# A layer that opens in the place of another's weights, and a seventh product on a shared bank

## The chip, the cores and the metric

The kernel runs on 1 core of one Trainium2 chip. The metric is the device time of one execution in microseconds (us), smaller is better. The kernel before takes 1030.41 us, the median of three runs (1029.31 to 1032.5).

## The reference, cut to what matters

Three layers follow one another: windowed attention, a gated layer, and a two-matrix layer with the mish function. The first two stay as they are in this case; the third, and the passage into it, is what the change is about.

```python
def _moe_ref(x, w_gate, w_val, w_out):        # 2304 tokens, 512 -> 1536 -> 512
    g = x @ w_gate
    silu = g * (1.0 / (1.0 + np.exp(-g)))
    val = x @ w_val
    return (silu * val @ w_out).astype(np.float32)

def _moe2_ref(x, w_in, w_out):                # 2304 tokens, 512 -> 2048 -> 512
    h = x @ w_in
    sp = np.where(h > 20.0, h, np.log1p(np.exp(np.minimum(h, 20.0))))
    g = h * np.tanh(sp)
    return (g @ w_out).astype(np.float32)
```

## The kernel before

**Numbers.** Every matrix product is made of three TensorE matmuls of 128 rows: an operand is split into a high part (ScalarE copies it to the type fp32r, `hi_act`, L124) and a low part (VectorE subtracts the high part, `lo_dve`, L127), and high by high, high by low and low by high are summed in one PSUM bank (`mm`, L117).

**First layer.** It works through five token chunks. A chunk has groups of gate and value matmuls (24 of them, into `g_ps`) and projections of 12 matmuls that add to four accumulators `acc`. The weights that a projection needs pass through a ring of two tiles: SP loads `cw`, ScalarE and VectorE make the two parts `ring`. A projection runs some groups after its gate and value group; in the last chunk `CFG["lastlag"]` sets by how much, and four projections (48 matmuls) stand behind the last gate and value group. They are called `carry` in the code. Then `evacuate` (L580, L581) copies the accumulators out, and SP writes them to the DRAM tensor `x2d`. While the first layer runs, other code makes the seven combined weights of layer two's second matrix and SP writes them to DRAM (`w2o`, L556). Its twelve weight tiles `w` of 8 KB per partition, its activations and its ring lie in pools of one stack, `sa`, which is closed when the last projection has been issued. Only then does the pool `bp` of layer two open.

**Second layer.** `layer2` takes three blocks p of 768 tokens. Both matrix products are done with seven products of half-size blocks instead of eight (a scheme of Strassen's kind), numbered 1 to 7. `load_x` reads a block of tokens from `x2d` into `xr` (two loads, L682), `x_parts` makes seven operand pairs `xs1` to `xs7` with four VectorE sums (L666, in `sums4`) in between. In the hidden part, eight tiles j each do the seven products in `ORDER1`, 6 matmuls each, with weights `win` which `make_win` makes from a raw tile `w4` (L745): four subtractions on GpSimd (L752) into the only tile `t4`, then two ScalarE copies and two VectorE subtractions. `outputs` sums the banks into four quarters of `G` and `mish` is applied to each. In the output part each of the seven products in `ORDER2` has two banks (m = 0, 1) and four operands `op` (q = 0 to 3), each used by 6 matmuls on one bank and 6 on the other, 48 matmuls for a product. `operands` makes them from `G`, with four VectorE sums for each q, and five `op` buffers go round; `load_wout` brings the weights. `bank()` hands out alternately one of four rotating banks and one of the four accumulators in turn.

Product 2 is added onto product 1's bank, so that the sum of 1 and 2 needs no addition. The other sums are VectorE's. What `outputs` does with a product's bank is this:

```python
if i == 1:   u["a"] = new(); nc.scalar.activation(out=u["a"], in_=bk, func=AF.Copy)
elif i == 6: add(u["a"], u["a"], bk)
elif i == 7: u["b"] = new(); add(u["b"], u["a"], bk)
elif i == 2: done(0, bk, None)
elif i == 5: add(u["a"], u["a"], bk); done(3, u["b"], bk)
elif i == 3: done(1, u["a"], bk)
else:        done(2, u["b"], bk)
```

In the output part product 4 comes first; its two banks are kept until `b` is there, and `done(2, u["b"], p4)` is called after product 7 (tile `y`).

**What sets the order.** TensorE's instructions run in the order in which they are written. On the other engines and on the DMA queues a scheduler orders them when the program is built. All loads and stores spoken of here are on the queue of SP.

Of the kernel before, what the change touches and what calls it, by code (L numbers as in the profile page):

```python
# [9 lines left out]
F32 = mybir.dt.float32  # L10
F32R = mybir.dt.float32r
# [85 lines left out]
def body(ctx: ExitStack, tc: tile.TileContext, qT, kT, vP, w1, w1o, w2, cst, yT):  # L97
    nc = tc.nc
    const = ctx.enter_context(tc.tile_pool(name="const", bufs=1))
    sa = ExitStack()  # L100
    wp = sa.enter_context(tc.tile_pool(name="wp", bufs=12))
    xp = sa.enter_context(tc.tile_pool(name="xp", bufs=2))
    hp_ = sa.enter_context(tc.tile_pool(name="hp", bufs=2))
    dr = ctx.enter_context(tc.tile_pool(name="dr", bufs=1, space=bass.MemoryType.DRAM))
# [354 lines left out]
        return wp.tile([128, 2, 1024], F32R, tag="w", name="w")  # L459

    def ring_tile():
        return wp.tile([128, 2, 1024], F32R, tag="ring", name="ring", bufs=2)

    stage = {}

# [199 lines left out]
    def add(out, a, b, op=ALU.add):  # L665
        nc.vector.tensor_tensor(out=out, in0=a, in1=b, op=op)  # L666
# [68 lines left out]
    def layer2(bp, mish):  # L735
        G = {}
        win, wout = {}, {}
        ORDER1 = (1, 6, 7, 2, 5, 4, 3)
        ORDER2 = (4, 1, 6, 7, 2, 5, 3)

        raws = {}

        def load_raw(p, j):
            raws[p, j] = bp.tile([128, 4, 256], F32, tag="w4", name="w4", bufs=2)
            nc.sync.dma_start(out=raws[p, j], in_=w2d[j].rearrange("p (k n) -> p k n", k=4))  # L745

        def make_win(p, j):

            w = raws.pop((p, j))
            x = bp.tile([128, 4, 256], F32, tag="t4", name="t4", bufs=1)  # L750
            for o, a, b in ((0, w[:, 0], w[:, 1]), (1, w[:, 3], x[:, 0]), (2, w[:, 3], w[:, 0]), (3, x[:, 1], w[:, 2])):
                nc.gpsimd.tensor_tensor(out=x[:, o], in0=a, in1=b, op=ALU.subtract)  # L752
            t = win[p, j] = bp.tile([128, 2, 7, 256], F32R, tag="win", name="win")
# [9 lines left out]
        def hidden(p, j, xs):  # L763
            w = win.pop((p, j))
            q, jj = divmod(j, 2)
            if jj == 0:
                G[p, q] = bp.tile([128, 4, 2, TB], F32, tag=f"g{q}", name="G", bufs=1)
            g = G[p, q]
            u = {}

            def new():
                return bp.tile([128, TB], F32, tag="u", name="u", bufs=6)

            def done(k, a, b):
# [6 lines left out]
            bk1 = None  # L781
            for i in ORDER1:
                bk = bk1 if i == 2 else bank()
                if i == 1:
                    bk1 = bk
                s = SLOT[i]
                products(
                    bk, [(w[:, 0, s, c:c + 128], w[:, 1, s, c:c + 128]) for c in (0, 128)],
                    [(xs[i][:, 0, c], xs[i][:, 1, c]) for c in range(2)], i != 2, i != 1,
                )  # L790
                outputs(i, bk, u, new, done)

        def operands(p, i):

            ops = []
# [12 lines left out]

        xr = load_x(bp, 0)
        for j in range(2):  # L810
            load_raw(0, j)
        xs = x_parts(bp, xr)
        for j in range(2):
            make_win(0, j)
            load_raw(0, j + 2)
        yr = yT.rearrange("(c p) t -> p c t", p=128)
        for p in range(NPB):
            loads = [(i, k) for i in ORDER2 for k in range(2)]
# [6 lines left out]
                    load_wout(p, *loads.pop(0))  # L825
                hidden(p, j, xs)
            if p + 1 < NPB:
                xr = load_x(bp, p + 1)
# [4 lines left out]
            bk1 = [None, None]  # L833
            left = [[2, 2], [2, 2]]
            t0 = 2 * p * TB
            for i in ORDER2:
                bks = bk1 if i == 2 else [bank(), bank()]
                if i == 1:
                    bk1 = bks
                for q, o in enumerate(operands(p, i)):  # L840
                    k, jq = divmod(2 * q, NJ // 2)
                    if (p, i, k) not in wout:
# [5 lines left out]
                    for m in range(2):  # L848
                        products(
                            bks[m],  # L850
                            [(w[:, jq + e, 0, 128 * m:128 * m + 128], w[:, jq + e, 1, 128 * m:128 * m + 128]) for e in range(2)],
                            [(o[:, 0, e], o[:, 1, e]) for e in range(2)],
                            i != 2 and q == 0, i != 1 and q == NJ // 2 - 1,
                        )
                for m in range(2):

# [19 lines left out]
                        done(2, us[m]["b"], us[m]["p4"])  # L876
                if p + 1 < NPB:
                    if i == 7:
                        xs = x_parts(bp, xr)
                    if i in (2, 5):  # L880
                        j = (2, 5).index(i)
                        make_win(p + 1, j)
                        load_raw(p + 1, j + 2)

    with tc.manual_schedule(engines={mybir.EngineType.PE}):
# [42 lines left out]
        for ci, p in enumerate(plansA):  # L928
# [27 lines left out]
            for gi, (kind, i, f) in enumerate(groups):  # L956
# [12 lines left out]
                while win and (spent * ng < (gi + 1) * total or gi == len(groups) - 1):  # L969
# [23 lines left out]
        layer2(bp, mish)  # L993


def _layouts(np, q, k, v, moe_w_gate, moe_w_val, moe_w_out, moe2_w_in, moe2_w_out):
# [45 lines left out]
```

## Time and profile before

| what | value |
|---|---|
| runs | 1029.31, 1030.41, 1032.5 us (median 1030.41) |
| profiled execution, its own time | 1030.16 us |
| span of its profile | 1027.5 us |
| mean granted TensorE clock | 0.975 |
| TensorE busy with matmuls | 979.5 us, 5168 matmuls |
| attention and first layer, until the last projection ends | about 632.8 us |
| second layer | the rest |

The span runs from the first to the last recorded instruction; the execution's own time is 2.66 us longer. Engines are named PE (TensorE), DVE (VectorE), ACT (ScalarE), POOL (GpSimd) and SP (the queue that issues DMAs). A row of a timeline gives the start, the length, the engine, the line, the operation, what it writes and reads, how many instructions were put together, and in brackets how long the engine had been idle and which work released it.

### The profile page before, as it was taken

The numbers are of one execution on the slowest core, as the hardware profiler recorded it, in microseconds if no ns is written. First come the engines' busy times: TensorE is split into PE (matmuls) and PEld (weight loads), VectorE is DVE, ScalarE is ACT, GpSimd is POOL, SyncE is SP. The second block draws the span as 40 slices with busy tenths as digits, with TensorE's granted clock in tenths as the row PEclk, the third lists the DMA queues.
The fourth block names the chain that finished last, engine by engine and source line by source line (L and its number), as shares of the span: only waits on it lengthen the run. The fifth ranks groups of instructions, "written<-read, shape, count | busy, mean of one in ns | idle before, by whom it ended". The sixth has DMA issues, their size and how long they took to land.

```text
span 1027.5 us, 14547 instructions
## 1 busy us (share of the span) xinstructions
PE 979.5 (95%) x5168; PEld 860.0 (84%) x5168; DVE 722.6 (70%) x1271; ACT 551.4 (54%) x1121; POOL 151.6 (15%) x204
## 2 busy tenths in 40 slices
PE   7899999999999999999999996699899998999998
PEld 5567677898987777788888996599899998999998
DVE  5998887777667644468534573888984889758773
ACT  7867655757666754455443442455542565335442
POOL 3600000000000000000002440653221332113000
PEclk7899999999999999999999998699999999999999
DMA  8853424475345621247304995423586136850175
GB/s 317 278 206 128 154 85 129 147 238 184 121 145 172 217 91 60 78 155 246 123 1 147 355 326 179 191 83 103 189 290 218 62 126 226 285 171 32 55 256 202
DMA packets 74936, 173.90 MB, mean 169 GB/s; under 512 B 8432, under 2 KB 50032, under 8 KB 65136
## 3 DMA queue, kind: packets, MB, share of 16 engines
q1 hardware_dynamic: 74864, 172.98, 49.5%
q8 instruction: 40, 0.66, 0.2%
q14 instruction: 32, 0.26, 0.1%
HBM read 137.30 MB, written 35.65 MB: 168 GB/s over the span
## 4 chain that ended last, share of the span: by engine, by line
PE 76%; DVE 8%; DMA 6%; ACT 4%; issue 3%; POOL 2%; SPq 1%; DVEq 0%; ACTq 0%; POOLq 0%
PE g_ps L117 27%; PE bk L117 24%; PE acc L117 13%; PE o_ps L117 5%; PE s_ps L117 4%; PE t_ps L259 3%; DMA wraw<-w 2%; POOL t L752 2%; DVE G L666 2%; ACT win L124 1%; DVE win L127 1%; DVE op L127 1%; DMA wout<-w2o 1%; DVE xr L666 1%; DVE u L666 1%
## 5 line engine op out<-in xcount | busy, mean ns | idle before, releaser
L117 PE MATMUL g_ps<-xt,w 128*128 128x512 f32 (+1 forms) x1440 | 317.2, 371 | 0.3 <-ACT PT L271 0.3
L117 PEld LDWEIGHTS g_ps<-xt,w 128*128 128x128 f32 x1440 | 258.2, 188 | 37.6 <-issue 3.3
L117 PE MATMUL bk<-xs,win 128*128 128x384 f32 x1008 | 182.7, 340 | 22.0 <-ACT win L124 10.5
L117 PEld LDWEIGHTS bk<-xs,win 128*128 128x128 f32 x1008 | 177.0, 191 | 27.4 <-ACT win L124 10.8
L117 PE MATMUL bk<-op,wout 128*128 128x384 f32 x1008 | 179.7, 338 | 7.2 <-DVE op L127 6.4
L117 PEld LDWEIGHTS bk<-op,wout 128*128 128x128 f32 x1008 | 177.4, 191 | 9.1 <-DVE op L127 7.7
L117 PE MATMUL acc<-hh,ring 128*128 128x512 f32 (+1 forms) x480 | 149.5, 373 | 0.0
L124 ACT ACTIVATE op<-G 128x768 fp32r<-128x768 f32 x84 | 69.7, 842 | 64.9 <-PE bk L117 49.6
L127 DVE TENSOR_TENSOR op<-G,op 128x768 fp32r<-128x768 f32 x84 | 82.8, 999 | 26.0 <-ACT op L124 25.5
L117 PEld LDWEIGHTS acc<-hh,ring 128*128 128x128 f32 x480 | 89.1, 188 | 13.6 <-issue 1.9
L117 PE MATMUL acc<-hl,ring 128*128 128x512 f32 (+1 forms) x240 | 88.4, 368 | 0.0
L752 POOL TENSOR_TENSOR t<-w 128x256 f32<-128x256 f32 x48 | 48.6, 1034 | 236.7 <-DVE win L127 206.5
L230 ACT ACTIVATE Pt<-Pt,sm 128x256 f32<-128x256 f32 (+2 forms) x160 | 74.5, 467 | 16.9 <-DVE sm L226 16.6
L226 DVE CUSTOM_DVE_ANT_0 Pt<-s_ps,cst_sb 128x256 f32<-128x256 f32 (+2 forms) x160 | 54.5, 376 | 31.3 <-PE s_ps L117 31.0
L603 DVE SCALAR_TENSOR_TENSOR t<-t,g_ps 128x512 f32<-128x512 f32 (+1 forms) x60 | 37.7, 628 | 52.0 <-ACT t L602 51.9
L602 ACT ACTIVATE t<-g_ps 128x512 f32<-128x512 f32 (+1 forms) x60 | 33.0, 551 | 75.1 <-PE g_ps L117 74.9
L611 DVE SCALAR_TENSOR_TENSOR t<-t,g_ps 128x512 f32<-128x512 f32 (+1 forms) x60 | 37.9, 632 | 41.6 <-PE g_ps L117 40.9
L124 ACT ACTIVATE hh<-t 128x512 fp32r<-128x512 f32 (+1 forms) x60 | 34.9, 581 | 51.6 <-DVE t L611 51.6
L541 POOL TENSOR_TENSOR cw<-cw 128x256 f32<-128x256 f32 x32 | 30.0, 962 | 191.2 <-DMA cw<-w2d 163.8
L209 POOL MEMSET sm<- 128x8 f32 x40 | 4.9, 135 | 336.8 <-ACT Pt L247 308.7
L247 ACT ACTIVATE Pt<-Pt,sm 128x256 f32<-128x256 f32 (+2 forms) x128 | 50.2, 465 | 7.9 <-DVE sm L241 7.8
L666 DVE TENSOR_TENSOR u<-u,bk 128x384 f32<-128x384 f32 x72 | 39.6, 550 | 20.6 <-PE bk L117 18.8
(71 smaller groups left out, 1318.2 us busy)
## 6 DMA issues: line engine op xcount, KB each, us to landing
wout<-w2o SPq DMA_DIRECT2D x42, 1024.0 KB, 5.2
wraw<-w SPq DMA_DIRECT2D x16, 1024.0 KB, 5.6
w2o<-chl SPq DMA_DIRECT2D x16, 896.0 KB, 6.6
wst<-w SPq DMA_DIRECT2D x12, 1024.0 KB, 8.1
cw<-w1od SPq DMA_DIRECT2D x24, 512.0 KB, 3.9
w<-w2d SPq DMA_DIRECT2D x24, 512.0 KB, 3.2
w2d<-cw SPq DMA_DIRECT2D x16, 512.0 KB, 4.2
wraw<-w1o SPq DMA_DIRECT2D x6, 1024.0 KB, 6.4
```

The costliest lines, as they stand in the source:

```text
L117: nc.tensor.matmul(out=out, lhsT=lhsT, rhs=rhs, start=start, stop=stop, skip_group_check=True)
L124: nc.scalar.activation(out=out, in_=in_, func=AF.Copy)
L127: nc.vector.tensor_tensor(out=out, in0=in_, in1=hi.bitcast(F32), op=ALU.subtract)
L226: nc.vector.tensor_tensor_reduce(out=Pt[:q.qn, :w], in0=s_ps[:q.qn, q.so:q.so + w], in1=nb[:q.qn, 128 - q.kn:128 + q.qn], op0=ALU.add, op1 ...
L230: nc.scalar.activation(out=Pt[:q.qn, :w], in_=Pt[:q.qn, :w], func=AF.Exp, scale=-1.0, bias=sm[:q.qn, i:i + 1], accum_out=sm[:q.qn, 8 + i:9 ...
L247: nc.scalar.activation(out=pt, in_=pt, func=AF.Copy, scale=r)
L259: nc.tensor.transpose(t_ps[:x.n, o:o + q.qn], Pt[:q.qn, c0:c0 + x.n], ident[:q.qn, :q.qn])
L602: tanhs.append(nc.scalar.activation(out=t[:, :n], in_=st["g"][:, :n], func=AF.Tanh, scale=0.5))
L603: nc.vector.scalar_tensor_tensor(out=t[:, :n], in0=t[:, :n], scalar=1.0, in1=st["g"][:, :n], op0=ALU.add, op1=ALU.mult)
L611: nc.vector.scalar_tensor_tensor(out=t[:, :n], in0=t[:, :n], scalar=0.5, in1=vps[:, :n], op0=ALU.mult, op1=ALU.mult)
L666: nc.vector.tensor_tensor(out=out, in0=a, in1=b, op=op)
L752: nc.gpsimd.tensor_tensor(out=x[:, o], in0=a, in1=b, op=ALU.subtract)
```

## The change

1. `lastlag` goes from 3 to 4: five projections instead of four stand behind the last gate and value group.
2. The first layer's weight tiles get a stack of their own, `sw`, on the other side of the memory (`side="right"`); the ring moves to the pool of activations. As soon as the last gate and value group has been issued, `sw` is closed and in its place a pool `br` opens for layer two's `w4`, `t4`, `win`, `xr` and `xs`. `layer2` becomes a generator: its first part (the first loads, `x_parts`, `make_win` for two tiles) is issued before the `carry` projections, the rest after them, when `bp` has been opened.
3. Product 3 is added onto product 5's bank, as product 2 is onto product 1's (`onto`). The addition `add(u["a"], u["a"], bk)` after product 5 goes away: 24 times in the hidden part, 6 times in the output part. Product 5 comes before product 2 in both orders.
4. In `operands` the four sums for each q stand after product 4's, 1's and 7's operands and ahead of 6's, instead of three ahead of 6's and one ahead of 3's.

```diff
-    order="SSOTT", delay0=2, early=[4], pbufs=10, pump_g=2, pump_p=2, lag=4, lastlag=3, evprio=500,
+    order="SSOTT", delay0=2, early=[4], pbufs=10, pump_g=2, pump_p=2, lag=4, lastlag=4, evprio=500,
...
-    sa = ExitStack()
-    wp = sa.enter_context(tc.tile_pool(name="wp", bufs=12))
+    sa, sw = ExitStack(), ExitStack()
+    wp = sw.enter_context(tc.tile_pool(name="wp", bufs=12, side="right"))
...
         if i == 1:
-            u["a"] = new()
-            nc.scalar.activation(out=u["a"], in_=bk, func=AF.Copy)
+            u["c"] = new()
+            nc.scalar.activation(out=u["c"], in_=bk, func=AF.Copy)
         elif i == 6:
+            u["a"] = u.pop("c")
             add(u["a"], u["a"], bk)
...
+        elif i == 5:
+            done(3, u["b"], bk)
         elif i == 2:
             done(0, bk, None)
-        elif i == 5:
-            add(u["a"], u["a"], bk)
-            done(3, u["b"], bk)
...
-        ORDER1 = (1, 6, 7, 2, 5, 4, 3)
-        ORDER2 = (4, 1, 6, 7, 2, 5, 3)
+        ORDER1 = (1, 6, 7, 5, 2, 4, 3)
+        ORDER2 = (4, 1, 6, 7, 5, 2, 3)
+        onto = {2: 1, 3: 5}
...
                 if i == 6:
+                    add(g[:, 0], g[:, 3], g[:, 0], ALU.subtract)
+                part(o, g[:, {4: 3, 1: 0, 6: 0, 7: 2, 2: 1, 5: 3, 3: 2}[i]])
+                yield o
+                if i == 4:
                     add(g[:, 3], g[:, 2], g[:, 3])
+                if i == 1:
                     add(g[:, 2], g[:, 0], g[:, 2], ALU.subtract)
-                    add(g[:, 0], g[:, 3], g[:, 0], ALU.subtract)
-                if i == 3:
-                    add(g[:, 1], g[:, 1], g[:, 0], ALU.subtract)
-                part(o, g[:, {4: 3, 1: 0, 6: 0, 7: 2, 2: 1, 5: 3, 3: 1}[i]])
-                ops.append(o)
-                yield o
+                if i == 7:
+                    add(g[:, 2], g[:, 1], g[:, 0], ALU.subtract)
...
         pump(10000)
+        sw.close()
+        br = ctx.enter_context(tc.tile_pool(name="br", bufs=3, side="right", reuse_waits="tile"))
+        second = layer2(br)
+        next(second)
         for f in carry:
             f()
```

**SP's queue where the first layer ends.** `chl` holds combined output weights, `ev` the last evacuated sums. Before, the last `w2o` write is followed by the two writes to `x2d`, and only then by the loads for layer two:

```order
L556 DMA w2o_75<-chl_5913 128x7x256
L582 DMA x2d_72<-ev_6050 128x2x384
L582 DMA x2d_72<-ev_6054 128x2x384
L682 DMA xr_6066<-x2d_72 128x4x384 x2
L745 DMA w4_6069<-w2d_74 128x1024
L745 DMA w4_6071<-w2d_74 128x1024
L761 DMA wout_6498<-w2o_75 128x2048
```

Now:

```order
L556 DMA w2o_75<-chl_5884 128x7x256
L747 DMA w4_6006<-w2d_74 128x1024
L682 DMA xr_6008<-x2d_72 128x4x384 x2
L747 DMA w4_6011<-w2d_74 128x1024
L747 DMA w4_6048<-w2d_74 128x1024
L582 DMA x2d_72<-ev_6110 128x2x384
L747 DMA w4_6060<-w2d_74 128x1024
L582 DMA x2d_72<-ev_6114 128x2x384
```

The loads of `xr` and of the first raw weights have moved ahead of the last two writes to `x2d`.

**DVE at the same place.** `hl` is the low part of the last activation of layer one. Before:

```order
L127 TENSOR_TENSOR hl_5999<-t_5978,hh_5998 128x384
L581 COPY ev_6050<-acc1_5549 128x384
L581 COPY ev_6054<-acc3_5551 128x384
L127 TENSOR_TENSOR xs1_6073<-xr_6066,xs1_6073 128x768
L127 TENSOR_TENSOR xs2_6074<-xr_6066,xs2_6074 128x768
L127 TENSOR_TENSOR xs4_6076<-xr_6066,xs4_6076 128x768
L666 TENSOR_TENSOR xr_6066<-xr_6066 128x768
L127 TENSOR_TENSOR win_6103<-w4_6069,win_6103 128x768
```

Now:

```order
L127 TENSOR_TENSOR hl_5982<-t_5964,hh_5981 128x384
L127 TENSOR_TENSOR ring_5999<-cw_5997,ring_5999 128x1024
L127 TENSOR_TENSOR win_6043<-w4_6006,win_6043 128x768
L127 TENSOR_TENSOR xs1_6013<-xr_6008,xs1_6013 128x768
L127 TENSOR_TENSOR xs2_6014<-xr_6008,xs2_6014 128x768
L127 TENSOR_TENSOR win_6043<-t4_6038,win_6043 128x1024
L127 TENSOR_TENSOR xs4_6016<-xr_6008,xs4_6016 128x768
L581 COPY ev_6110<-acc1_5593 128x384
L666 TENSOR_TENSOR xr_6008<-xr_6008 128x768
L127 TENSOR_TENSOR win_6055<-w4_6011,win_6055 128x768
L581 COPY ev_6114<-acc3_5595 128x384
L666 TENSOR_TENSOR xr_6008<-xr_6008 128x768
```

Five operations for layer two and the last ring tile now stand ahead of the first evacuation. Behind these rows follow, in the kernel now, the low part of `xs5`, that of `win_6055` from `t4_6050`, a sum, that of `xs7`, a sum, and that of `xs6`.

**PE and DVE in the output part of block 0, from product 7 to the next.** Before, PE goes from product 7 (`bk_6915`, `bk_6916`) to product 2, on the banks of product 1:

```order
L117 MATMUL bk_6916<-op_6966,wout_6843 128x384 x6
L117 MATMUL bk_6765<-op_7012,wout_6881 128x384 [waits DMAHW4_49,Activation_49]
L117 MATMUL bk_6765<-op_7012,wout_6881 128x384 [waits DVE_49]
L117 MATMUL bk_6765<-op_7012,wout_6881 128x384 x4
L117 MATMUL bk_6766<-op_7012,wout_6881 128x384 x6
```

Now it goes to product 5, on two banks handed out anew (`bk_7004` is the accumulator that product 4 has held as `bk_6687`):

```order
L117 MATMUL bk_6903<-op_6956,wout_6836 128x384 x6
L117 MATMUL bk_7003<-op_7005,wout_6870 128x384 [waits DMAHW4_49,DVE_49,Activation_49]
L117 MATMUL bk_7003<-op_7005,wout_6870 128x384 [waits DVE_49]
L117 MATMUL bk_7003<-op_7005,wout_6870 128x384 x4
L117 MATMUL bk_7004<-op_7005,wout_6870 128x384 [waits DVE_49]
L117 MATMUL bk_7004<-op_7005,wout_6870 128x384 x5
```

The wait ahead of `bk_7004` is for the row that writes `y_6683` in DVE's order there:

```order
L127 TENSOR_TENSOR op_7054<-G_6554,op_7054 128x768
L666 TENSOR_TENSOR v_6972<-v_6826,bk_6902 128x384
L666 TENSOR_TENSOR v_6975<-v_6828,bk_6903 128x384
L127 TENSOR_TENSOR op_7083<-G_6137,op_7083 128x768
L666 TENSOR_TENSOR y_6682<-v_6972,bk_6686 128x384
L666 TENSOR_TENSOR y_6683<-v_6975,bk_6687 128x384
```

`op_7083` is the first operand of product 2, in the buffer that product 7's last operand `op_6956` leaves. Block 1 reads the same; in block 2 its row stands between the two `y`.

## Rows read from the trace of the kernel before

**Rows 1.** Page, part 1: busy time, share of the span, instructions.

```profile
PE 979.5 (95%) x5168; PEld 860.0 (84%) x5168; DVE 722.6 (70%) x1271; ACT 551.4 (54%) x1121; POOL 151.6 (15%) x204
```

**Rows 2.** Waits of PE from 650 us on: total us, times, longest us.

```profile
PE bk L117 <- DVE op L127: 6.4, 4, 2.5
PE bk L117 <- ACT u L719: 2.9, 7, 1.3
PE bk L117 <- DMA wout<-w2o: 0.8, 1, 0.8
```

**Rows 3.** PE's timeline at the passage between the layers.

```profile
632.45 0.34 PE L117 MATMUL acc<-hh,ring 128*128 128x384 f32 x1
643.32 1.01 PE L117 MATMUL bk<-xs,win 128*128 128x384 f32 x2 [10.53 <-ACT win L124]
...
655.17 11.51 PE L117 MATMUL bk<-xs,win 128*128 128x384 f32 x53 [3.24 <-DVE xs L127]
```

**Rows 4.** Windows: length, busy of PE, PEld, DVE, ACT, POOL, PEclk, DMA share, GB/s.

```profile
633.00:643.00 10.00, 0.00 (x0) 0.00 (x0) 3.17 (x4) 3.00 (x4) 0.47 (x1) 0.64 1.00 361
643.00:655.00 12.00, 3.34 (x7) 1.92 (x7) 11.99 (x10) 5.70 (x8) 8.15 (x7) 0.50 0.70 289
655.00:667.00 12.00, 11.51 (x53) 11.19 (x53) 8.53 (x12) 5.44 (x9) 6.98 (x8) 0.81 0.25 88
```

**Rows 5.** SP's timeline: the last w2o writes and the loads of xr.

```profile
605.87 10.69 SPq L556 DMA_DIRECT2D w2o<-chl  x4
...
633.90 1.29 SPq L682 DMA_DIRECT2D xr<-x2d  x2
```

**Rows 6.** ACT's timeline there.

```profile
638.98 1.58 ACT L124 ACTIVATE xs<-xr 128x768 fp32r<-128x768 f32 x2 [6.12 <-DMA xr<-x2d]
...
657.14 1.06 ACT L124 ACTIVATE win<-t 128x1024 fp32r<-128x1024 f32 x1 [2.55 <-POOL t L752]
```

**Rows 7.** The chain in order of time: start, us, what.

```profile
624.46 8.34 PE acc L117 x48
```

**Rows 8.** DVE's timeline at the passage.

```profile
631.78 0.56 DVE L581 COPY ev<-acc 128x384 f32<-128x384 f32 x1 [5.57 <-PE acc L117]
...
649.37 0.94 DVE L666 TENSOR_TENSOR xr<-xr 128x768 f32<-128x768 f32 x1
650.24 1.21 DVE L127 TENSOR_TENSOR win<-t,win 128x1024 fp32r<-128x1024 f32 x1
651.38 0.94 DVE L127 TENSOR_TENSOR xs<-xr,xs 128x768 fp32r<-128x768 f32 x1
652.25 1.47 DVE L666 TENSOR_TENSOR xr<-xr 128x768 f32<-128x768 f32 x1
653.64 2.88 DVE L127 TENSOR_TENSOR xs<-xr,xs 128x768 fp32r<-128x768 f32 x2
```

**Rows 9.** POOL's timeline there: the subtractions of two tiles.

```profile
651.53 2.77 POOL L752 TENSOR_TENSOR t<-w 128x256 f32<-128x256 f32 x2 [3.77 <-DVE win L127]
...
655.78 1.33 POOL L752 TENSOR_TENSOR t<-t,w 128x256 f32<-128x256 f32 x1
659.54 2.16 POOL L752 TENSOR_TENSOR t<-w 128x256 f32<-128x256 f32 x2 [2.43 <-DVE win L127]
...
662.47 0.73 POOL L752 TENSOR_TENSOR t<-t,w 128x256 f32<-128x256 f32 x1
```

**Rows 10.** Page, part 5: sums into u; count, busy, mean ns, idle before.

```profile
L666 DVE TENSOR_TENSOR u<-u,bk 128x384 f32<-128x384 f32 x72 | 39.6, 550 | 20.6 <-PE bk L117 18.8
```

**Rows 11.** DVE's timeline in layer two: sums into G, and one operand.

```profile
719.22 0.54 DVE L666 TENSOR_TENSOR G<-u,bk 128x384 f32<-128x384 f32 x1
...
739.50 0.94 DVE L127 TENSOR_TENSOR op<-G,op 128x768 fp32r<-128x768 f32 x1
...
927.55 1.48 DVE L666 TENSOR_TENSOR G<-u,bk 128x384 f32<-128x384 f32 x3
```

**Rows 12.** PE's timeline in the output parts of blocks 0 and 2.

```profile
737.89 43.60 PE L117 MATMUL bk<-op,wout 128*128 128x384 f32 x239 [2.49 <-DVE op L127]
...
965.25 58.41 PE L117 MATMUL bk<-op,wout 128*128 128x384 f32 x336
```

More of the change, by code (lines that the diff above doesn't have):

```diff
@@ L461, in ring_tile @@
     def ring_tile():
-        return wp.tile([128, 2, 1024], F32R, tag="ring", name="ring", bufs=2)
+        return hp_.tile([128, 2, 1024], F32R, tag="ring", name="ring", bufs=2)
     stage = {}
@@ L733, in outputs, with layer2 @@
             done(2, u["b"], bk)
-    def layer2(bp, mish):
+    def layer2(br):
         G = {}
         win, wout = {}, {}
-        ORDER1 = (1, 6, 7, 2, 5, 4, 3)
-        ORDER2 = (4, 1, 6, 7, 2, 5, 3)
+        ORDER1 = (1, 6, 7, 5, 2, 4, 3)
+        ORDER2 = (4, 1, 6, 7, 5, 2, 3)
+        onto = {2: 1, 3: 5}
         raws = {}
         def load_raw(p, j):
-            raws[p, j] = bp.tile([128, 4, 256], F32, tag="w4", name="w4", bufs=2)
+            raws[p, j] = br.tile([128, 4, 256], F32, tag="w4", name="w4", bufs=2)
             nc.sync.dma_start(out=raws[p, j], in_=w2d[j].rearrange("p (k n) -> p k n", k=4))
@@ L749, in make_win @@
             w = raws.pop((p, j))
-            x = bp.tile([128, 4, 256], F32, tag="t4", name="t4", bufs=1)
+            x = br.tile([128, 4, 256], F32, tag="t4", name="t4", bufs=1)
             for o, a, b in ((0, w[:, 0], w[:, 1]), (1, w[:, 3], x[:, 0]), (2, w[:, 3], w[:, 0]), (3, x[:, 1], w[:, 2])):
                 nc.gpsimd.tensor_tensor(out=x[:, o], in0=a, in1=b, op=ALU.subtract)
-            t = win[p, j] = bp.tile([128, 2, 7, 256], F32R, tag="win", name="win")
+            t = win[p, j] = br.tile([128, 2, 7, 256], F32R, tag="win", name="win")
             for d, src in ((slice(0, 3), w[:, 1:4]), (slice(3, 7), x)):
@@ L779, in done @@
                 mish(g[:, k, jj], g[:, k, jj])
-            bk1 = None
+            bks = {}
             for i in ORDER1:
-                bk = bk1 if i == 2 else bank()
-                if i == 1:
-                    bk1 = bk
+                bk = bks[i] = bks[onto[i]] if i in onto else bank()
                 s = SLOT[i]
@@ L788, in hidden @@
                     bk, [(w[:, 0, s, c:c + 128], w[:, 1, s, c:c + 128]) for c in (0, 128)],
-                    [(xs[i][:, 0, c], xs[i][:, 1, c]) for c in range(2)], i != 2, i != 1,
+                    [(xs[i][:, 0, c], xs[i][:, 1, c]) for c in range(2)], i not in onto, i not in onto.values(),
                 )
@@ L793, in operands @@
         def operands(p, i):
-            ops = []
             for q in range(NJ // 2):
@@ L799, in operands @@
                 if i == 6:
+                    add(g[:, 0], g[:, 3], g[:, 0], ALU.subtract)
+                part(o, g[:, {4: 3, 1: 0, 6: 0, 7: 2, 2: 1, 5: 3, 3: 2}[i]])
+                yield o
+                if i == 4:
                     add(g[:, 3], g[:, 2], g[:, 3])
+                if i == 1:
                     add(g[:, 2], g[:, 0], g[:, 2], ALU.subtract)
-                    add(g[:, 0], g[:, 3], g[:, 0], ALU.subtract)
-                if i == 3:
-                    add(g[:, 1], g[:, 1], g[:, 0], ALU.subtract)
-                part(o, g[:, {4: 3, 1: 0, 6: 0, 7: 2, 2: 1, 5: 3, 3: 1}[i]])
-                ops.append(o)
-                yield o
[L809 to L812, printed above, removed]
+                if i == 7:
+                    add(g[:, 2], g[:, 1], g[:, 0], ALU.subtract)
+        load_raw(0, 0)
+        xr = load_x(br, 0)
+        load_raw(0, 1)
+        xs = x_parts(br, xr)
         for j in range(2):
@@ L815, in layer2 @@
             load_raw(0, j + 2)
+        bp, mish = yield
         yr = yT.rearrange("(c p) t -> p c t", p=128)
@@ L827, in layer2 @@
             if p + 1 < NPB:
-                xr = load_x(bp, p + 1)
+                xr = load_x(br, p + 1)
                 for j in range(2):
@@ L832, in layer2 @@
             ys = [[bp.tile([128, 2, TB], F32, tag="y", name="y", bufs=4) for _ in range(2)] for _ in range(2)]
-            bk1 = [None, None]
+            held = {}
             left = [[2, 2], [2, 2]]
@@ L836, in layer2 @@
             for i in ORDER2:
-                bks = bk1 if i == 2 else [bank(), bank()]
-                if i == 1:
-                    bk1 = bks
+                bks = held[i] = held[onto[i]] if i in onto else [bank(), bank()]
                 for q, o in enumerate(operands(p, i)):
@@ L852, in layer2 @@
                             [(o[:, 0, e], o[:, 1, e]) for e in range(2)],
-                            i != 2 and q == 0, i != 1 and q == NJ // 2 - 1,
+                            i not in onto and q == 0, i not in onto.values() and q == NJ // 2 - 1,
                         )
@@ L878, in layer2 @@
                     if i == 7:
-                        xs = x_parts(bp, xr)
-                    if i in (2, 5):
-                        j = (2, 5).index(i)
+                        xs = x_parts(br, xr)
+                    if i in (5, 2):
+                        j = (5, 2).index(i)
                         make_win(p + 1, j)
@@ L992, in body @@
         bp = ctx.enter_context(tc.tile_pool(name="bp", bufs=3, reuse_waits="tile"))
-        layer2(bp, mish)
+        try:
+            second.send((bp, mish))
+        except StopIteration:
+            pass
 def _layouts(np, q, k, v, moe_w_gate, moe_w_val, moe_w_out, moe2_w_in, moe2_w_out):
```

## The prediction

> **What bounds the kernel now.** I read the page first: PE is busy in 95% of the span, DVE in 70% [rows 1]. The matmuls are the same in number after the change, so only PE's idle time and its clock can give anything. Then the waits of PE in layer two [rows 2] and PE's timeline at the passage [rows 3], where one stretch stands out: the first layer's last matmul ends at 632.79, the first product of layer two starts at 643.32 after 10.53 us without work, and steady work, from product 6 of the first tile on, begins only at 655.17. These 22.4 us hold six matmuls of product 1 and the first of product 6. [...]
>
> The passage begins with a load. SP issues `xr` at 633.90, behind the writes to `x2d` [rows 5]; ACT's first `xs` copy waits for it until 638.98 [rows 6]. From there DVE sets the pace, busy in 11.99 of 12.00 us [rows 4].
>
> Elsewhere in layer two PE waits little: 6.4 us for operands `op` (four times), 2.9 us in seven waits for ACT's copy of product 1 (`u`), 0.8 us for a `wout` load [rows 2].
>
> **The change, part by part.**
>
> *Earlier loads.* `xr` and the raw weights stand ahead of the `x2d` writes on SP. The w2o writes in front of them leave SP at 616.56 (605.87 + 10.69) [rows 5], and the weight tiles whose place they take are free when the last gate and value groups end. Those now end one projection earlier: 48 matmuls of 8.34 us follow them today, ending at 632.8 [rows 7], 0.174 us each, so 60 need 10.4 us and the last group ends at 622.2 instead of 624.3. The load of `xr` took 5.1 us from issue to ACT's first use (633.90 to 638.98); issued at 617 to 622 it is there by 622 to 627. I take it that it no longer decides; bound below: 3 us later.
>
> *DVE's queue.* What then counts is DVE's order: the low part of the last ring tile, of `win`, `xs1`, `xs2`, of the `t4` part of `win`, of `xs4`. The ring tile is free when the projection two back has ended, about 624.4, and ACT's copy of that shape takes 1.06 [rows 6], so with a queue before it DVE starts at about 626.05. From start to start a 128x768 operation takes 0.87 (649.37 to 650.24), a 128x1024 one 1.14 (650.24 to 651.38) [rows 8]; 2 x 1.14 + 4 x 0.87 = 5.8, so `xs4` ends at 631.8, just as `acc` is to be evacuated [rows 8].
>
> GpSimd starts on the second tile's `t4` when DVE has read the first, at about 631.1. Beside DVE its four subtractions took 5.58 us (651.53 to 655.78 + 1.33), later 3.66 (659.54 to 662.47 + 0.73) [rows 9]. I take 5.58, as DVE is busy: 636.7. ACT copies it until 637.8, and DVE's low part with its 1.21 ends at 639.0; the operations in front of it (two evacuations, two sums, two low parts) fill 631.8 to 636.4 and are done. Behind it stand a sum, `xs7`, a sum, `xs6`. Before, the last three took from 652.25 - 0.87 to about 655.1, that is 3.65, and a sum beside GpSimd took 1.4 (652.25 to 653.64) [rows 8]: 5.1 us, and product 6 starts at **644.1 instead of 655.2: -11.1 us**. With GpSimd at 3.66 and nothing slowed it would be 641.0 (-14.2); with `xr` late by 3 us, 647.2 (-8.0). PE still idles some 10 us, so I leave its way back to full clock as it was [rows 4].
>
> What slows DVE there is GpSimd: 1.4 against 0.87 for one operation [rows 8], 0.53 us more. [...]
>
> *One addition less.* 30 additions into `u` of 0.55 us go (24 hidden, 6 output) [rows 10], 16 us of DVE time. As DVE is waited for in few places, I count nothing for the time itself.
>
> *Product 3 on 5's bank, hidden part.* Product 3 must now wait until DVE has added 5's bank into `G`. Products 2 and 4 stand between: 12 matmuls, 2.08 us at 0.174. An addition takes 0.54, a row of three 1.48 [rows 11]. Where DVE also makes weights or operands (two tiles of eight in each block, I count j = 2 and j = 4), the addition comes later; a low part of 1.21 and one of 0.94 [rows 8] ahead of it, then 0.54, is 2.7, so 0.5 us is lost: 6 x 0.5 = +3.0. In turn product 2 comes one product later, and the 2.9 us of waits for ACT's `u` [rows 2] should go. **Net +0.1** (-2.9 to +3).
>
> *Sums spread.* Ahead of the second operand of product 6 DVE now has four operations instead of two behind the first one, in two blocks. Today this operand (739.50 [rows 11]) is late already, and PE has stood 2.49 us before product 6 [rows 12]. Some 0.4 us more each: **+0.8** (0 to 2). Block 2 runs 336 matmuls in 58.41 us without a gap [rows 12], so it has nothing to gain.
>
> *A new wait in the output part.* Before, product 7 was followed by product 2, on banks it already had, 48 matmuls of 8.3 us. Now product 5 follows, on two new banks, and the second is the accumulator that product 4 holds until `y` is formed. DVE's order there: `v` twice, the low part of an operand, `y` twice. That operand takes the buffer of product 7's last operand, so ACT can copy only when product 7 ends (0.8, as a `xs` copy of that shape, 1.58 for two [rows 6]), then DVE subtracts (0.94 [rows 8]), then two `y` of 0.5: the second is done 3.0 us after product 7's end, with 0.2 of start-up each time. PE needs the bank after 6 matmuls, 1.04 us. Stall 2.0 us in blocks 0 and 1, and 1.6 in block 2 where one `y` is ahead of the operand: **+5.6** (4 to 7). Five more operands queue behind, but PE has 42 matmuls, 7.3 us, to let them catch up.
>
> *Sum.* -11.1 + 0.1 + 0.8 + 5.6 = -4.6. The profiled execution took 1030.16, so 1025.6; the median of the runs is 0.25 higher, so **1025.8**. About 0.3%, 3.1 us, is what a measurement of this kernel can tell from no change: faster means below 1027.3, slower above 1033.5.
>
> **Rivals.**
>
> *A. The passage closes further.* GpSimd and DVE get out of each other's way (3.66 instead of 5.58 [rows 9]): -14.2; product 2's waits end and only half of product 3's new ones come (-1.4); the bank wait is at the low end (+4.1). -11.5: 1018.9. For it: 0.87 against 1.4 in the same stretch [rows 8]. Against: DVE has no gap there.
>
> *B. The loads don't come early.* The change doesn't do what it says if SP, or the transfers behind it, hold `xr` and the raw weights: the DMA share is 1.00 after 633 [rows 4]. If they land 4 us later than I take it, product 6 starts at 648: -7.1 + 6.5 = -0.6, 1029.8. Against: nothing but the w2o writes is in front, and these are out by 616.56 [rows 5].
>
> *C. Product 3 waits everywhere* (the other side: slower). If DVE's addition of 5 ends later than 2.08 us after product 5 in every tile, 24 tiles lose some 0.5 us: +12, less the 2.9 of `u`. -11.1 + 12 - 2.9 + 0.8 + 5.6 = +4.4: 1034.8. It decides where two other DVE operations stand ahead of the addition. For it: at 927.55 three additions run one after the other, so they had queued [rows 11]. Against: most tiles have few other DVE operations; a lone addition takes 0.54. [...]
>
> **How the numbers follow.** The forecast has 0.50; with its terms' bounds its own range is 1022 to 1029, so 0.34 of it is faster and 0.16 the same. A has 0.22, all faster. B has 0.17: 0.06 faster, 0.09 the same, 0.02 slower. C has 0.11: 0.09 slower, 0.02 the same. Faster 0.62, same 0.27, slower 0.11. The range takes in A at 1018 and B up to 1030; C and the edges, under 0.2, are left out.
>
> **What would show it.** Right: in the profile after, `xr` is issued before 623; PE's steady work in layer two begins near 644; DVE is nearly full from 626 to there; between product 7 and product 5 in each output part PE waits 1.6 to 2.0 us for DVE `y`; PE waits for ACT `u` are gone and some short ones for DVE `G` have come, in two tiles of eight. Wrong: steady work before 641 or after 647, a wait for `G` in nearly every tile, or none for `y`.

## The result, and the profile after

The changed kernel takes 1038.9 us, the median of four runs (1037.21 to 1040.23); the kernel before took 1030.28 us over its four runs by then. The ratio is 1.008, with a 95% interval of 1.0057 to 1.0102: slower by 8.6 us, where 1025.8 us was forecast, and outside the range.

The profiled execution of the changed kernel took 1040.23 us, the longest of the four, with a span of 1038.4 us against 1027.5 before. The main waits of PE from 640 us on (total us, times, longest) stand against [rows 2]:

```profile
PE bk L117 <- DVE y L666: 12.7, 3, 5.8
PE bk L117 <- ACT xs L124: 6.9, 1, 6.9
PE bk L117 <- DVE op L127: 6.6, 5, 2.0
PE bk L117 <- DVE xs L127: 2.6, 1, 2.6
PE bk L117 <- DVE G L666: 2.2, 6, 0.5
```

The waits for ACT's `u` are gone, six short ones for `G` have come, and there are three for `y`: the forecast had each of these. But `y` is 12.7 us where 5.6 were taken. PE's timeline has the three of them, one in each output part; the first row is the work that ends where the first wait begins (747.34 + 5.31 = 752.65):

```profile
747.34 5.31 PE L117 MATMUL bk<-op,wout 128*128 128x384 f32 x29 [1.25 <-DVE op L127]
758.04 26.26 PE L117 MATMUL bk<-op,wout 128*128 128x384 f32 x138 [5.39 <-DVE y L666]
...
889.00 25.65 PE L117 MATMUL bk<-op,wout 128*128 128x384 f32 x138 [5.81 <-DVE y L666]
...
1010.11 24.20 PE L117 MATMUL bk<-op,wout 128*128 128x384 f32 x138 [1.53 <-DVE y L666]
```

PE's timeline at the passage, against [rows 3]:

```profile
640.21 0.34 PE L117 MATMUL acc<-hh,ring 128*128 128x384 f32 x1
640.39 1.22 PE L117 MATMUL bk<-xs,win 128*128 128x384 f32 x6
648.56 0.69 PE L117 MATMUL bk<-xs,win 128*128 128x384 f32 x1 [6.95 <-ACT xs L124]
651.88 16.34 PE L117 MATMUL bk<-xs,win 128*128 128x384 f32 x80 [2.63 <-DVE xs L127]
```

From the end of layer one (640.55) to steady work (651.88) it is now 11.33 us, before it was 22.38. The forecast had 11.3. But layer one ends 7.76 us later than before, at 640.55 instead of 632.79, and of that the forecast had nothing.

The matmuls are the same in number and order up to the last chunk, so the two traces can be laid side by side, matmul by matmul. The difference after minus before, in the traced executions (a part goes from its first matmul to the next part's first):

| stretch | difference, us |
|---|---|
| start until matmul 200 (about 60 us) | +3.51 |
| from there to the end of layer one | +4.25 |
| end of layer one to steady work | -11.05 |
| hidden parts behind that | -2.1 |
| output parts of blocks 0, 1, 2: +7.74, +6.45, +1.83 | +16.0 |
| behind the last matmul | +0.3 |
| span | +10.9 |

The first entry belongs to the execution: in the fourteen traces of this study matmul 200 starts between 60.1 and 64.0 us, and kernels whose first 600 us are instruction for instruction alike lie 3.8 us apart there. Of the losses, the second and the fifth are the change's.

### The profile page after: what moved, and what is told of

Same layout as the page of the kernel before. It is cut to its first block, busy times and chain, and to the rows that moved or that the text cites. A ratio compares the mean times of both kernels' runs of the same rounds, so it can differ in the third digit from the quotient of the medians.

```text
span 1038.4 us, 14510 instructions
## 1 busy us (share of the span) xinstructions
PE 985.0 (95%) x5168; PEld 863.1 (83%) x5168; DVE 701.0 (68%) x1241; ACT 550.9 (53%) x1121; POOL 180.1 (17%) x204
## 4 chain that ended last, share of the span: by engine, by line
PE 76%; DVE 9%; POOL 5%; DMA 5%; ACT 2%; issue 1%; SPq 1%; DVEq 0%; POOLq 0%; ACTq 0%
PE g_ps L117 28%; PE bk L117 23%; PE acc L117 13%; PE o_ps L117 5%; POOL t L754 5%; PE s_ps L117 4%; PE t_ps L259 3%; DVE G L666 2%; DVE op L127 2%; DVE win L127 2%; DMA w2d<-cw 1%; POOL Pt L249 1%; DMA wst<-w 1%; DVE xs L127 1%; DMA wraw<-w1o 1%
## 5 line engine op out<-in xcount | busy, mean ns | idle before, releaser
L117 PE MATMUL g_ps<-xt,w 128*128 128x512 f32 (+1 forms) x1440 | 322.0, 375 | 0.3 <-ACT PT L271 0.3
L117 PE MATMUL bk<-op,wout 128*128 128x384 f32 x1008 | 183.5, 342 | 19.5 <-DVE y L666 12.7
L117 PEld LDWEIGHTS bk<-op,wout 128*128 128x128 f32 x1008 | 179.5, 193 | 23.0 <-DVE y L666 13.7
L117 PE MATMUL bk<-xs,win 128*128 128x384 f32 x1008 | 179.9, 338 | 11.8 <-ACT xs L124 6.9
L754 POOL TENSOR_TENSOR t<-w 128x256 f32<-128x256 f32 x48 | 82.9, 1747 | 209.7 <-DVE win L127 198.1
L230 ACT ACTIVATE Pt<-Pt,sm 128x256 f32<-128x256 f32 (+2 forms) x160 | 74.6, 468 | 17.4 <-DVE sm L226 16.9
L666 DVE TENSOR_TENSOR G<-u,bk 128x384 f32<-128x384 f32 x72 | 39.3, 552 | 36.5 <-PE bk L117 34.4
L993 ACT ACTIVATE G<-G 128x384 f32<-128x384 f32 x72 | 37.0, 518 | 49.8 <-DVE G L666 49.8
```

The lines of the kernel that those rows point to most:

```text
L117: nc.tensor.matmul(out=out, lhsT=lhsT, rhs=rhs, start=start, stop=stop, skip_group_check=True)
L230: nc.scalar.activation(out=Pt[:q.qn, :w], in_=Pt[:q.qn, :w], func=AF.Exp, scale=-1.0, bias=sm[:q.qn, i:i + 1], accum_out=sm[:q.qn, 8 + i:9 ...
```

## The experiments

### Layer one: where the weights lie

The second entry is not one late wait but a pace. The chain of the kernel before, then that of the changed kernel: one group of 24 gate and value matmuls of the last chunk (start, us, what).

```profile
620.30 4.16 PE g_ps L117 x24
```

```profile
625.91 4.24 PE g_ps L117 x24
```

That is 0.1733 and 0.1767 us for a matmul. The matmuls on `ring`, `win` and `wout` keep their 0.173 us from start to start, also in the changed kernel. What the change did to the first layer is to move tiles: the twelve weight tiles `w` went from the bottom of the left side to the right side, and `xt`, the activations that the same matmuls read (pool `xp`), came down from above `w` and the ring to the bottom of the left side. The expectations below call the left side low and the right side high.

**Run e1**: the kernel before with `wp` on the right side in a stack of its own and the ring in `hp`, nothing else.

```diff
-    wp = sa.enter_context(tc.tile_pool(name="wp", bufs=12))
+    wp = sw.enter_context(tc.tile_pool(name="wp", bufs=12, side="right"))
...
-        return wp.tile([128, 2, 1024], F32R, tag="ring", name="ring", bufs=2)
+        return hp_.tile([128, 2, 1024], F32R, tag="ring", name="ring", bufs=2)
```

> The kernel before with one thing of the change: the weight tiles w (and the tiles that use their pool) lie on the other side of the memory, the ring with the activations; every engine has the order of before. Theory (place): with xt low and w high the gate and value matmuls run at 0.176 instead of 0.1735 us (384 columns) and 0.233 instead of 0.228 us (512 columns), as in the changed kernel, so layer one ends 4 to 8 us later: 1034 to 1038 us. Rival (the later end of layer one is of that execution or comes with the other parts): 1030 us, last projection ending near 632.8.

1035.35 us, ratio 1.0049 (1.0035 to 1.0064). The group of 24 takes 4.24 us; from matmul 200 to the end of layer one it is 4.3 us more than before. The place alone slows the layer.

**Run e2**: the changed kernel mirrored: `wp` and `br` on the left, `xp`, `hp`, `att`, `cv` and `bp` on the right.

```diff
-    wp = sw.enter_context(tc.tile_pool(name="wp", bufs=12, side="right"))
-    xp = sa.enter_context(tc.tile_pool(name="xp", bufs=2))
+    wp = sw.enter_context(tc.tile_pool(name="wp", bufs=12))
+    xp = sa.enter_context(tc.tile_pool(name="xp", bufs=2, side="right"))
...
```

> The changed kernel with the two sides exchanged (w and the pool br on the left, all else on the right); every engine has the order of the changed kernel. Theory (place, xt low with w high is the slow pair): the gate and value matmuls are back at 0.1735 us, layer one ends near 633, 1031 us. Rival (any two sides are slow for a pair that lies apart): layer one as slow as in the changed kernel, 1038 to 1039 us. The waits for y stay at some 5.5, 5.5 and 1.7 us under both.

1035.69 us, ratio 1.0048 (1.0028 to 1.0067): 3.2 us less than the changed kernel by the medians. The group of 24 is at 4.16 us, the stretch at 572.8 us (before 572.3, changed 576.6), the waits for `y` at 12.7 as they were. The time is above the 1031 expected, because that took the whole 7.7 us for the place's. The intervals of the two ratios overlap (the changed kernel's begins at 1.0057), so it is the pace in the trace that shows the effect.

**Run e5**: the kernel before with the two pools opened in the other order, so that `xt` lies at the bottom and `w` directly above it.

```diff
-    wp = sa.enter_context(tc.tile_pool(name="wp", bufs=12))
     xp = sa.enter_context(tc.tile_pool(name="xp", bufs=2))
+    wp = sa.enter_context(tc.tile_pool(name="wp", bufs=12))
```

> The kernel before with xt and the weight tiles w exchanged in place on the same side: xt at the bottom, w directly above it; every engine has the order of before. Theory (a matmul is slower where its moving operand lies below its weights): the gate and value matmuls take 0.176 (384 columns) and 0.233 us (512), the stretch from matmul 200 to the end of layer one is 576 instead of 572.3 us, 1035 us. Rival (xt and w must lie in different halves of the memory to be slow): 0.1735 and 0.2285 us, 572 us, 1031 us.

1030.11 us, ratio 1.0 (0.9985 to 1.0016), 4.16 us for the 24. My theory fell here: `xt` below `w` is not slow by itself.

**Run e9**: run e1 with `xt` on the right too, above `w`.

```diff
-    wp = sw.enter_context(tc.tile_pool(name="wp", bufs=12, side="right"))
-    xp = sa.enter_context(tc.tile_pool(name="xp", bufs=2))
+    xp = sw.enter_context(tc.tile_pool(name="xp", bufs=2, side="right"))
+    wp = sw.enter_context(tc.tile_pool(name="wp", bufs=12, side="right"))
```

> Run e1 with xt on the high side too, above the weight tiles. Theory (slow is xt low with w high, and only that pair): the gate and value matmuls are back at 0.1735 (384 columns) and 0.2285 to 0.2295 us (512), matmul 200 to the end of layer one 572 to 573 us, 1030 to 1031.5 us. Rival (weights on the high side are slow wherever xt lies): 0.176 and 0.233 us, 576.5 us, 1035 us.

The group takes 4.19 us and the stretch 573.1 us, most of the way back. The time is not: 1035.58 us, ratio 1.0047 (1.0034 to 1.0061). In its trace the passage is 2.0 us longer than before (`xr` is issued 3.2 us after layer one's end, before 1.1); the other losses are about a microsecond each: the start, layer one, the output parts. So the matmul's pace follows the pair of places, and the time of this kernel isn't explained by it.

Of the four pairs that were tried, only `xt` low with `w` high is slow (4.24 us for the 24, the others 4.16 to 4.19). Why was not found out.

### The output part: order, banks and sums

**Run e3**: the changed kernel with the output part's order and banks of before.

```diff
-        ORDER2 = (4, 1, 6, 7, 5, 2, 3)
+        ORDER2 = (4, 1, 6, 7, 2, 5, 3)
         onto = {2: 1, 3: 5}
+        onto2 = {2: 1}
...
         elif i == 5:
+            if apart:
+                add(u["a"], u["a"], bk)
             done(3, u["b"], bk)
```

(`onto2` in place of `onto` in the output part, `apart` true there; the next block's weights are made behind products 2 and 5 as before.)

> The changed kernel with the output part's product order and banks of before (product 2 behind 7 on the banks of 1, product 3 on banks of its own, the addition after 5 back). Theory (new banks behind product 7 cause the waits for y): 12.7 us of waits for y go, and the slow-clock stretches behind the two long ones with them, 1024 to 1026 us. Rival (VectorE is late there whatever the banks): waits for op of 3 us or more in each of blocks 0 and 1 take their place, 1031 us or more.

1024.04 us, ratio 0.9939 (0.9913 to 0.9964): faster than the kernel before, and 14.9 us below the changed one. No wait for `y` is left and none for `op` takes its place (5.6 us in four).

**Run e4**: the changed kernel with the operand sums of before.

```diff
                 if i == 6:
+                    add(g[:, 3], g[:, 2], g[:, 3])
+                    add(g[:, 2], g[:, 0], g[:, 2], ALU.subtract)
                     add(g[:, 0], g[:, 3], g[:, 0], ALU.subtract)
+                if i == 3:
+                    add(g[:, 1], g[:, 1], g[:, 0], ALU.subtract)
...
-                if i == 4:
-                    add(g[:, 3], g[:, 2], g[:, 3])
-                if i == 1:
-                    add(g[:, 2], g[:, 0], g[:, 2], ALU.subtract)
-                if i == 7:
-                    add(g[:, 2], g[:, 1], g[:, 0], ALU.subtract)
```

> The changed kernel with the operand sums where they were (three ahead of product 6's operands, one ahead of 3's). Theory (the long waits for y in blocks 0 and 1 come from a GpSimd subtraction that a run of VectorE operations without a gap holds back for 19 us, and the sums' new places make that run): the subtraction takes under 3 us, the waits for y are near 2.0 us, 1031 to 1033 us. Rival (the banks alone): the waits for y stay near 5.5 us in blocks 0 and 1, 1038 to 1040 us.

1031.27 us, ratio 1.001 (0.9995 to 1.0025), 7.6 us below the changed kernel. PE's waits from 640 us on:

```profile
PE bk L117 <- DVE y L666: 7.7, 3, 3.3
PE bk L117 <- ACT xs L124: 6.9, 1, 6.9
PE bk L117 <- DVE op L127: 3.9, 2, 2.0
```

The time came as the theory said, its reason did not: GpSimd's subtraction still lasts 18.8 us in both blocks, and DVE still stands 3.9 us for the weight behind it. DVE's row in block 0 of e4:

```profile
740.35 1.22 DVE L127 TENSOR_TENSOR win<-t,win 128x1024 fp32r<-128x1024 f32 x1 [3.93 <-ACT win L124]
```

With that pause left in place, the waits for `y` in blocks 0 and 1 have fallen to 3.3 us at most. What the sums' places do is seen in the changed kernel itself, in block 0. DVE's timeline, then POOL's and ACT's rows that stand before it:

```profile
738.92 0.95 DVE L666 TENSOR_TENSOR G<-G 128x768 f32<-128x768 f32 x1
743.78 1.23 DVE L127 TENSOR_TENSOR win<-t,win 128x1024 fp32r<-128x1024 f32 x1 [3.91 <-ACT win L124]
744.92 0.95 DVE L666 TENSOR_TENSOR G<-G 128x768 f32<-128x768 f32 x1
745.79 2.90 DVE L127 TENSOR_TENSOR op<-G,op 128x768 fp32r<-128x768 f32 x2
748.61 1.00 DVE L666 TENSOR_TENSOR v<-v,bk 128x384 f32<-128x384 f32 x2
749.54 1.38 DVE L127 TENSOR_TENSOR op<-G,op 128x768 fp32r<-128x768 f32 x1
750.84 1.81 DVE L666 TENSOR_TENSOR G<-G 128x768 f32<-128x768 f32 x2
752.58 2.68 DVE L127 TENSOR_TENSOR op<-G,op 128x768 fp32r<-128x768 f32 x3
755.19 1.00 DVE L666 TENSOR_TENSOR v<-v,bk 128x384 f32<-128x384 f32 x2
756.11 0.94 DVE L127 TENSOR_TENSOR op<-G,op 128x768 fp32r<-128x768 f32 x1
756.98 1.00 DVE L666 TENSOR_TENSOR y<-v,bk 128x384 f32<-128x384 f32 x2
```

```profile
720.84 20.32 POOL L754 TENSOR_TENSOR t<-w 128x256 f32<-128x256 f32 x2 [8.63 <-DVE win L127]
```

```profile
742.69 1.06 ACT L124 ACTIVATE win<-t 128x1024 fp32r<-128x1024 f32 x1 [6.28 <-POOL t L754]
```

Read from the bottom. `y` is done at 757.98 and PE goes on at 758.04. PE had ended the first six matmuls of product 5 at 752.65, so product 7 at about 751.6; yet `v`, which needs only that, starts at 755.19, because DVE is behind: three operands of product 5 (2.68) and two sums (1.81) stand ahead. These were late because DVE had stood 3.91 us for a weight that ACT could copy only at 742.69, after GpSimd; and GpSimd's first subtraction, begun at 720.84 (20.32 us for two, of which the second has 0.73), ended 0.6 us after DVE's first pause in 19 us: DVE had run without a gap until 739.87. A late load is not behind it: the subtraction's raw weights were issued at 707.32, and such a load lands within 4.7 us.

**Run e10** takes GpSimd out of that chain.

```diff
-                nc.gpsimd.tensor_tensor(out=x[:, o], in0=a, in1=b, op=ALU.subtract)
+                (nc.vector if j == 2 and p else nc.gpsimd).tensor_tensor(out=x[:, o], in0=a, in1=b, op=ALU.subtract)
```

> The changed kernel with the four subtractions of tile j = 2 of blocks 1 and 2, the ones that GpSimd ends 20 us after their start, on VectorE. Theory (GpSimd held back by VectorE's run makes the weights late, VectorE stands 3.9 us for them in front of the sums that y waits behind): VectorE's idle time ahead of the low part of that tile goes, the waits for y in blocks 0 and 1 fall from 5.4 to 5.8 us to 2 to 3.3 us, 1031 to 1034 us. Rival (the two operand sums and the operands queued ahead of y make the wait): it stays above 4.5 us in both, 1037 us or more.

1031.3 us, ratio 1.0005 (0.9991 to 1.002): 7.6 us below the changed kernel. PE's timeline in blocks 0 and 1 (a row with the rest of product 6, product 7 and product 5's first six matmuls, then the row behind the wait):

```profile
731.61 15.70 PE L117 MATMUL bk<-op,wout 128*128 128x384 f32 x89 [2.30 <-DVE op L127]
751.90 18.33 PE L117 MATMUL bk<-op,wout 128*128 128x384 f32 x96 [4.59 <-DVE y L666]
...
859.33 17.29 PE L117 MATMUL bk<-op,wout 128*128 128x384 f32 x89 [2.32 <-DVE op L127]
879.61 10.69 PE L117 MATMUL bk<-op,wout 128*128 128x384 f32 x60 [2.98 <-DVE y L666]
```

Block 1 is where the theory wanted it, block 0 at the rival's bound: DVE's 3.9 us pause is gone, yet the two sums and the operands ahead of `v` still fill the queue there. Both causes work, and either of them taken away gives 7.6 us. Not all of that is the wait for `y`: in the traces product 7 of blocks 0 and 1, which takes 9.85 and 10.75 us in the changed kernel because PE waits for its operands, is down to 8.73 and 8.32 in e4 and to 8.32 twice in e10.

### The version that is left, and its parts

**Run e6** joins e2, e3 and e4: mirrored, output part and sums of before. What is left of the change is the early opening and the hidden part.

> The changed kernel with the sides exchanged, the output part's order and banks of before and the operand sums of before: what is left of the change is the early opening of layer two and the hidden part's product 3 on 5's bank. Theory (the parts add): run e3's 1024.0 less 3.5 us for layer one's matmuls and less up to 2.4 us of waits ahead of product 7's operands: 1018 to 1021 us. Rival (the sums and the order work against each other): 1022 to 1024 us.

1016.13 us, ratio 0.9868 (0.9849 to 0.9887): 14 us faster than the kernel before.

**Run e7** is e6 with `lastlag=3`.

> Run e6 with lastlag 3. Theory (the weights' place comes free 2.08 us earlier with lastlag 4, and VectorE's chain starts that much earlier): 1.5 to 2.5 us slower than e6. Rival (VectorE or GpSimd sets the passage from another point): within 0.5 us of e6.

1019.63 us, ratio 0.9905 (0.9882 to 0.9928): 3.5 us slower than e6, where 1.5 to 2.5 were expected. In the traces the passage gives 2.4 of them: from layer one's end to steady work it is 13.74 us against 11.35 in e6, the 2.08 us of one projection and a little more. The rest was not followed.

**Run e8** is e6 with the hidden part of before.

> Run e6 with the hidden part of before as well (product 3 on its own bank, the addition after 5 back, product 2 behind 7): only the early opening of layer two is left. Theory (product 3 on 5's bank is worth little: the waits for u of 2.9 us go and waits for G of 2.2 us come): 0 to 1 us slower than e6. Rival (24 additions less on VectorE pay beyond those waits): 2 to 4 us slower than e6.

1020.12 us, ratio 0.9906 (0.9889 to 0.9923): 4.0 us above e6, while the two traces differed by 0.3 us behind the passage. Both went again, side by side.

> Run e6 again beside the next one, on one chip with more rounds: 1016 to 1018 us.

> Run e8 again beside e6's. Their traces differ by 0.3 us behind the passage, their medians by 4.0 us. Theory (the hidden part is worth what the traces show): within 1.5 us of e6b. Rival (24 additions less pay in most executions, and the traced ones were unlike the rest): 3 to 4 us slower than e6b.

1016.87 us (ratio 0.9864, 0.9849 to 0.9879) and 1019.15 us (0.9885, 0.9867 to 0.9904): 2.3 us apart, between the two expectations. The second pair of traces differs by 3.25 us behind the passage. PE's waits from 640 us on in e6b, then in e8b:

```profile
PE bk L117 <- DVE op L127: 5.0, 4, 2.0
PE bk L117 <- DVE xs L127: 2.6, 1, 2.6
PE bk L117 <- DVE G L666: 2.2, 6, 0.5
PE bk L117 <- DMA wout<-w2o: 1.1, 2, 0.6
```

```profile
PE bk L117 <- DVE op L127: 6.6, 5, 2.5
PE bk L117 <- DVE xs L127: 2.6, 1, 2.6
PE bk L117 <- DMA wout<-w2o: 1.6, 2, 0.8
PE bk L117 <- ACT u L720: 1.5, 6, 0.2
```

So the hidden part is worth some 2 to 4 us by the medians, and the second pair's intervals overlap. In the hidden parts of blocks 1 and 2 it is 0.25 us a block; in the second pair the rest lies in the output parts, where DVE comes earlier to the operands: the wait for product 6's second operand is 2.0 instead of 2.5 us. In the first pair the output parts don't show it (186.35 us in e6, 185.43 in e8). In e6b product 6 took 10.8 us in both blocks, in e6 12.35, in e8 and e8b 11.6 to 12.7 (8.3 without a wait). The wait is 2.0 us in e6b and in e6 alike; behind it the granted clock was 1.00 in e6b (727.65 to 733) and 0.67 in e6 (728.78 to 734). The trace of the changed kernel has both: behind the 1.98 us that PE stands for that operand in block 0 the clock was 0.69 (733.50 to 739), behind the 1.99 us in block 1 it was 1.00 (864 to 870). So the clock falls there at some times and not at others, which also says why one trace was no measure of this part.

## Why the prediction was wrong

The range was 1018 to 1030, and the sum -4.6 us. By its steps:

- **Earlier loads and DVE's queue, -11.1.** Measured -11.05; the traces with the opening and lastlag 4 all have 11.7 to 11.9 us from the start of layer one's last matmul to steady work (before 22.7). Right, with its reason: `xr` was issued 16.7 us before layer one's end, and the row that ends the wait is DVE's `xs`, behind sums and low parts of 1.4 to 1.5 us beside GpSimd:

```profile
647.54 1.48 DVE L127 TENSOR_TENSOR xs<-xr,xs 128x768 fp32r<-128x768 f32 x1
648.95 1.47 DVE L666 TENSOR_TENSOR xr<-xr 128x768 f32<-128x768 f32 x1
650.35 2.87 DVE L127 TENSOR_TENSOR xs<-xr,xs 128x768 fp32r<-128x768 f32 x2
```

  From start to start that is 1.40 to 1.41 us, 0.53 to 0.54 more than the 0.87 without GpSimd. In the kernel before it was 0.53 as well. Steady work began at 651.88, outside the 641 to 647 that the prediction named, only because layer one ended 7.76 us later.
- **Product 3 on 5's bank, hidden part, +0.1 (-2.9 to +3).** The waits were as taken: six for `G` of at most 0.5 us, 2.2 in all, where 3.0 were counted; those for `u` are gone. Measured -2.1 in the traced hidden parts, inside the bounds; rival C (a wait in every tile) did not come. But 1.6 of the 2.1 lie in block 0 right behind the passage, and that is not shown to be this term's: from steady work to the output part it is 62.25 us before, 61.42 and 60.89 in e8 and e8b, which have the old hidden part, and 60.71 and 61.30 in e6 and e6b. Its own share in the hidden parts is some 0.2 us in each of the other two blocks.
- **Sums spread, +0.8.** Place and size were wrong, because it was counted alone. Product 6, where it was looked for, took 12.31 and 10.77 us in blocks 0 and 1 (before 12.67 and 12.39); what grew is product 7, from 8.32 to 9.85 and 10.75. With the old order of the output part the new sums cost less: product 7 takes 9.86 and 9.21 us in e3 and 8.32 in e6, which has the old sums, though e3's output parts as a whole take 187.1 us, 186.35 in e6 and 186.65 before. With the new order they cost 7.6 us (changed kernel against e4).
- **A new wait in the output part, +5.6 (4 to 7). This is the step that failed most.** The place, the bank and the waiting instruction were right. The size was not: waits of 5.39, 5.81 and 1.53 us (forecast 2.0, 2.0, 1.6), and product 5 took 17.1 us more than it should in all. It was right for block 2, where DVE makes no operands and weights for a next block. In blocks 0 and 1 the forecast let `v` start when product 7 ends; DVE got to it 3.6 us later in block 0 and 4.0 in block 1, since operands of product 5 and moved sums stood ahead of it. They stand in DVE's order right above the rows that front the prediction (the two sums at 750.84 and the operands at 752.58 in the trace); I counted what is behind `v` and not what is before it. GpSimd's late weight, which run e10 took away, was in no term either. The 0.2 of start-up stood there without a row. In the trace before, ACT's copy at 758.33, which waits for the matmuls on its buffer, starts 0.20 us after PE has gone on to the next matmul (758.14); in block 2 of the changed kernel DVE starts 0.03 us behind ACT's copy (1006.38) and PE 0.06 us behind `y` (1010.11). And the price of a wait was taken as the wait alone. The clock in block 0 behind it (window, us, busy of PE, PEld, DVE, ACT, POOL, PEclk, DMA share, GB/s):

```profile
752.70:758.00 5.30, 0.00 (x0) 0.00 (x0) 5.29 (x8) 0.00 (x0) 0.00 (x0) 0.78 0.55 187
758.00:762.40 4.40, 4.36 (x14) 4.36 (x15) 0.96 (x1) 0.84 (x1) 0.00 (x0) 0.50 0.00 0
762.60:772.00 9.40, 9.40 (x55) 9.40 (x55) 4.76 (x6) 3.54 (x5) 0.00 (x0) 1.00 0.67 219
```

PE idles 5.3 us, then works 4.4 us at a granted clock of 0.50, which is another 2.2 us lost; in block 1 product 5 took 1.7 us beyond its wait and the 8.32 of a product without one. In block 2, with 1.53 us of idling, PE's clock stays at 1.00 (1008.60 to 1014.00).

- **Layer one: not in the sum at all, measured +4.25.** The change part by part left out that the pools' move gives every tile of layer one another address; I read the new stack as a matter of when memory comes free. Run e1 shows that this alone costs 0.5%. Why the place slows a matmul stays open.
- **Spread of the rivals.** The three rivals concerned the passage and the hidden part. None had the output part's wait at more than the sum's own bounds, although that was the one new dependency on an engine that was busy 70% of the time.

Without the two terms of the output part the sum would have been -11.0 us; run e6, which has the early opening and the hidden part alone, gave -14. Three small workings of the prediction are off and decide nothing: 632.8 less 10.4 is 622.4 and not 622.2, 2.7 less 2.08 is 0.6 and not 0.5, and from 652.25 - 0.87 to 655.1 it is 3.7 and not 3.65.

## What to carry to other kernels

When a bank or buffer is to be given back earlier, price the wait from the row at which the freeing engine's queue stands then, by counting what is ahead of the freeing instruction as well as behind it; and add the stretch of slow clock behind a wait of several microseconds (here 2.2 us behind a wait of 5.4, none behind one of 1.5). A sum moved "where there is time" is queued ahead of something: its price belongs to the instruction that now comes behind it. And a change of pools is a change of addresses: compare the pace of matmuls that the change never touches (here 4.24 us instead of 4.16 for 24 of them).

## What the hardware showed unexpectedly

- A matmul's pace depended on where its two operands lie. Gate and value matmuls of 384 columns took 0.1767 instead of 0.1733 us (24 in 4.24 and 4.16), those of 512 columns 0.2333 instead of 0.2267 (24 in 5.60 and 5.44), when the weights lay on the right side and the moving operand at the bottom of the left one. Both on the left, both on the right (e9, 0.1746 and 0.2283 us) and the mirrored pair (e2, 0.1733 and 0.229) were fast or nearly so. Weights and moving operand of layer two's hidden part, both on the right side in the changed kernel, ran at 0.173.
- A GpSimd subtraction of two SBUF tiles, 0.73 us when alone (741.93 in the changed kernel, with DVE idle), lasted 19.6 us beside 22 DVE operations without a gap between them, each with two SBUF inputs, and ended 0.6 us after the first gap; DVE was not slowed (0.87 from start to start). In other places both engines took longer side by side: at 647.54 to 650.35 a DVE operation took 1.40 us from start to start and GpSimd 2.77 us for two subtractions (646.84). When both are slowed and when GpSimd alone is held was not settled. The long subtraction came with both orders of the sums (19.6 us in the changed kernel, 18.8 in e4) and, by the busy time, with the output order of before: the 48 rows `t<-w` of GpSimd add up to 82.9 us in the changed kernel and 81.2 in e6b. The kernel before has 48.6. In e6b no wait for `y` came of it. That DVE's run is what held GpSimd is read from the times, 0.6 us from the gap to the end in the changed kernel and in e4 alike; no run changed that run of DVE's alone.
